# Gate taps of later blocks ahead of the gated products: a lead of up to six taps, three buffers for gated tiles, and one group's conv units a block earlier

## The chip, the cores and the metric

The kernel runs on one core of a Trainium2 chip. Its engines are called here by their full names and, in rows, by short ones: TensorE (PE, with PEld for the loading of weights), VectorE (DVE), ScalarE (ACT), GpSimd (POOL) and SyncE (SP), which issues most transfers. The metric is the device time of one execution in microseconds (us), as the median of several executions.

## The reference

For 8 sequences of 4224 positions and 192 channels in float32, the reference does two things one after the other.

```python
# 1: every head (24 channels) is averaged over 7 positions with its own softmax weights
out = np.einsum('hk,bskhg->bshg', softmax(weight), windows(x))
# 2: on that result, a causal filter of 5 taps per channel makes a gate
for k in range(5):
    gate_pre += conv_w[k] * xp[:, k:k + S, :]
gate = 1 / (1 + exp(-gate_pre))
val = x @ w_val                     # 192 x 192
return (gate * val) @ w_out         # 192 x 192
```

Every position thus needs the averaged x, four multiply-adds and one multiplication for the gate, a product with w_val, a multiplication by the gate, and a product with w_out.

## The kernel before

**Data.** The channels lie on the partitions, 128 of them in "main" tiles and the remaining 64 of two streams of sequences in a "third" tile, so that a block of 502 positions (a few have 448, 500, 304, 302 or 188) is one tile of 128 x 2 x 502 (x1, index 0 and 1) and one of 128 x 502 (x2, index 2). There are 36 blocks, n = 0 to 35. They come in 14 groups; groups 4 to 11 have three blocks each (blocks 8 to 31), group 12 is blocks 32 and 33, group 13 is blocks 34 and 35.

**Conv units.** The 7-position average of a group is made by TensorE as products with a band matrix (`conv_unit`, L312), four windows to a unit. ScalarE copies a unit's PSUM bank to SBUF (tile `e`, L321), and SyncE then scatters it into the group's x1 and x2 (L350). The list `todo` says how many units the loop does at the end of block n: 4, 3, 3 in the three blocks of a group (4 in blocks 8, 11, 14, 17, 20, 23), and 2 in each of blocks 26 to 31; none later. The last six units, those of group 13, stand in blocks 29 to 31.

**A block.** All engines follow the order in which the code is written. In block n:
- TensorE: `diagonal` (L447) starts v of the third tile and o of block n-1's third tile, `main` (L457) starts v of tiles 0 and 1, `columns` (L485) ends v and o of the third tile, `rows` (L470) ends v of tiles 0 and 1 and starts o of tiles 0 and 1 of block n-1, `main` ends those, and then the conv units follow. v is the product with w_val, o the product with w_out. All are computed from a high and a low part of each operand, except for `columns`.
- VectorE: four taps (L391) on the gate accumulator `pa` of block n+1 (128 x 1004), then the three gated products (L504: v times gate, third tile first, then tiles 0 and 1), then four taps on `pb` of block n+1 (128 x 502).
- ScalarE: it closes a gate accumulator (`gate_close`, sigmoid from PSUM to SBUF, L404) and opens the next one in the same bank (`gate_open`, first tap, L384); it casts x and the gated products to their high parts (L412, L420; GpSimd subtracts for the low parts, L413, L421); it copies o out (`project`, L520), and the conv units (L321).

**Buffers.** The accumulators `pa` and `pb` have one buffer each: taps of a gate can start only after ScalarE has closed the one before and opened it. The gated tiles have two buffers (`gp`). All other PSUM tiles share five banks (`ps`): in a block these are v of tile 2, o of tile 2, v of 0, v of 1, o of 0, o of 1 and one per conv unit, asked for in this order. A bank comes free when ScalarE has copied a unit or an o tile, or when VectorE has made the gated product from a v tile.

Of the kernel before, what the change touches and what calls it, by code (L numbers as in the profile page):

```python
# [17 lines left out]
NH, KW, HC, KG = 8, 7, 24, 5  # L18
# [42 lines left out]
NG = len(NJS)  # L61
# [13 lines left out]
N = len(STEPS)  # L75
# [19 lines left out]

HEAD = 4

SOON = {2: (0, 2), 3: (1, 3), 4: (3, 5), 5: (5, 8)}


@with_exitstack
def kernel(
# [12 lines left out]
    ep = ctx.enter_context(tc.tile_pool(name="ep", bufs=EBUFS))  # L115
    xp = ctx.enter_context(tc.tile_pool(name="xp", bufs=3))
    sp = ctx.enter_context(tc.tile_pool(name="sp", bufs=2))
    gp = ctx.enter_context(tc.tile_pool(name="gp", bufs=2))
    pp = ctx.enter_context(tc.tile_pool(name="pp", bufs=2))
    op = ctx.enter_context(tc.tile_pool(name="op", bufs=3))  # L120
    ps_g = ctx.enter_context(tc.tile_pool(name="ps_g", bufs=1, space=PSUM))
# [10 lines left out]
    for g, n in enumerate(NJS):  # L132
        k = PER_LOAD[n]
# [164 lines left out]
    def conv_unit(u):  # L298
        g, q, ws = units[u]
        n = NJS[g]  # L300
        if u == first_unit[g]:
            x1s[g] = xp.tile([128, 2 * XB], F32, tag="x1", name=f"x1_{g}")
            x2s[g] = xp.tile([128, XC], F32, tag="x2", name=f"x2_{g}")
        if ws[0] == (0, 0):
            es[g, q] = ep.tile([M, 4 * NMAX * WIN], F32, tag="e", name=f"e_{g}_{q}")
        e = es[g, q]
        pc = ps.tile([128, 512], F32, tag="p", name=f"pc_{u}")
        for k, (hi, j) in enumerate(ws):
            h = QUADS[q][hi]
            i, at = home[g, h]  # L310
            c = (at * n + j) * M
            nc.tensor.matmul(  # L312
                pc[:M, k * WIN : (k + 1) * WIN],
                lhsT=xtiles[i][:, c : c + M],
                rhs=band[:, 4 * q + hi, :],
                start=True,
                stop=True,
            )
        a = (ws[0][0] * n + ws[0][1]) * WIN
        w = len(ws) * WIN  # L320
        nc.scalar.copy(e[:, a : a + w], pc[:M, :w])  # L321
        done = [hi for hi, j in ws if j == n - 1]
        for hi in done:
            h = QUADS[q][hi]
            i, at = home[g, h]
            last = at == len(loads[i][1]) - 1
            if last and g >= BY_POOL:
                load_x(allowed(i))
            scatter(g, h, e[:, hi * n * WIN : (hi + 1) * n * WIN])
            if last and g < BY_POOL:  # L330
                load_x(allowed(i))
# [33 lines left out]
    def views(n, k=KG - 1):  # L365
        g, o, m = STEPS[n]
        b = second(NJS[g])
        x1v = x1s[g][:, : 2 * b].rearrange("p (a t) -> p a t", a=2)
        return x1v[:, :, o + k : o + k + m], x2s[g][:, o + k : o + k + m]
# [5 lines left out]
    def gate_open(n, i):  # L375
        if n >= N:
            return
        m = STEPS[n][2]
        if i == 0:
            acc = ps_g.tile([128, 2, 512], F32, tag="pa", name=f"pa_{n}")[:, :, :m]  # L380
        else:
            acc = ps_h.tile([128, 512], F32, tag="pb", name=f"pb_{n}")[:, :m]
        accs[n, i] = acc
        nc.scalar.mul(acc, views(n, 0)[i], cwt[:, i, 0:1])  # L384

    def gate_taps(n, i, k0=1, k1=KG):
        if n >= N:
            return
        acc = accs[n, i]
        for k in range(k0, k1):  # L390
            nc.vector.scalar_tensor_tensor(  # L391
                out=acc, in0=views(n, k)[i], scalar=cwt[:, i, k : k + 1],
                in1=acc, op0=ALU.mult, op1=ALU.add,
            )

    def gate_close(n, i):
        if n >= N:
            return
        m = STEPS[n][2]
        if i == 0:  # L400
            dst = g1s[n] = gp.tile([128, 2, MB], F32, tag="g1", name=f"g1_{n}")[:, :, :m]
        else:
            dst = g2s[n] = gp.tile([128, MB], F32, tag="g2", name=f"g2_{n}")[:, :m]
        nc.scalar.activation(dst, accs.pop((n, i)), AF.Sigmoid)  # L404
# [3 lines left out]
    def split1(pool, tag, n, x):  # L408
        m = STEPS[n][2]
        h = pool.tile([128, 2, MB], F32R, tag="h", name=f"{tag}h_{n}")[:, :, :m]  # L410
        l = pool.tile([128, 2, MB], F32R, tag="l", name=f"{tag}l_{n}")[:, :, :m]
        nc.scalar.copy(h, x)  # L412
        nc.gpsimd.tensor_tensor(out=l, in0=x, in1=h.bitcast(F32), op=ALU.subtract)  # L413
        return h, l
# [11 lines left out]
    def bank(what, n, q):  # L426
        t = ps.tile([128, 512], F32, tag="p", name=f"{what}_{n}_{q}")[:, : STEPS[n][2]]
        banks[what, n, q] = t
        return t

    def operands(what, n):
        return (w_val, *xs[n, 1], *xs[n, 2]) if what == "v" else (w_out, *pr[n, 1], *pr[n, 2])

    def parts(w, h, l):
        return (w.h, h), (w.l, h), (w.h, l)

    def ok(n):
        return 0 <= n < N

    def diagonal(what, n):  # L440
        if not ok(n):
            return
        acc = bank(what, n, 2)
        w, _, _, h2, l2 = operands(what, n)
        r = slice(W22, W22 + 128)
        for i, (a, b) in enumerate(parts(w, h2, l2)):
            nc.tensor.matmul(acc, lhsT=a[:, r], rhs=b, start=(i == 0), stop=False)  # L447

    def main(what, n, q):
        if not ok(n):  # L450
            return
        fresh = (what, n, q) not in banks
        acc = bank(what, n, q) if fresh else banks[what, n, q]
        w, h, l, _, _ = operands(what, n)
        r = slice(W11, W11 + 128)
        for i, (a, b) in enumerate(parts(w, h, l)):
            nc.tensor.matmul(  # L457
                acc, lhsT=a[:, r], rhs=b[:, q], start=(fresh and i == 0), stop=(not fresh and i == 2)
            )
# [14 lines left out]
    def columns(what, n):  # L474
        if not ok(n):
            return
        m = STEPS[n][2]
        acc = banks[what, n, 2]
        w = w_val if what == "v" else w_out
        x = views(n)[0] if what == "v" else g1s[n]  # L480
        cuts = [m * i // 4 for i in range(5)]
        for i in range(4):
            c = slice(cuts[i], cuts[i + 1])
            for q, p in enumerate(HALVES):
                nc.tensor.matmul(  # L485
                    acc[p, c], lhsT=w.f[:, W12 : W12 + 64], rhs=x[:, q, c],
                    start=False, stop=(i == 3),
                )

    def split(n):  # L490
        if n >= N:
            return
        x1, x2 = views(n)
        if n == 0:
            xs[n, 2] = split2(sp, "x", n, x2)
        xs[n, 1] = split1(sp, "x", n, x1)
        if n > 0:
            xs[n, 2] = split2(sp, "x", n, x2)

    def gated(n, q):  # L500
        if not ok(n):
            return
        v = g1s[n][:, q] if q < 2 else g2s[n]
        nc.vector.tensor_tensor(out=v, in0=banks.pop(("v", n, q)), in1=v, op=ALU.mult)  # L504

    def split_gated1(n):
        if ok(n):
            pr[n, 1] = split1(pp, "p", n, g1s[n])

    def split_gated2(n):  # L510
        if ok(n):
            pr[n, 2] = split2(pp, "p", n, g2s[n])
# [22 lines left out]
    def conv(k):  # L535
        for _ in range(k):
            if done[0] < len(units):
                conv_unit(done[0])
                done[0] += 1

    todo = [0] * (N + 1)
    for g in range(LAG, NG):
        a, b = SOON.get(g) or (first[g - LAG], first[g - 1])
        k = first_unit[g + 1] - first_unit[g]
        for i in range(k):
            todo[a + i * (b - a) // k] += 1
# [24 lines left out]
    for n in range(HEAD):  # L571
        k = 2 if n < 2 else 3
# [21 lines left out]
        now = todo[n] if n == 0 else todo[n] // 2  # L594
# [6 lines left out]
        gate_close(n + 1, 1)  # L601
        gate_open(n + 2, 1)

    for n in range(HEAD, N + 1):
        diagonal("v", n)
        gate_taps(n + 1, 0, 1, 3)
        split(n + 1)
        diagonal("o", n - 1)
        main("v", n, 0)
        main("v", n, 1)  # L610
        gate_taps(n + 1, 0, 3, KG)
        columns("v", n)
        gated(n, 2)
        gate_close(n + 1, 0)
        gate_open(n + 2, 0)
        columns("o", n - 1)
        split_gated2(n)
        project(n - 1, 2)
        rows("v", n)
        gated(n, 0)  # L620
        gated(n, 1)
        rows("o", n - 1)
        split_gated1(n)
        main("o", n - 1, 0)
        gate_taps(n + 1, 1)
        project(n - 1, 0)
        main("o", n - 1, 1)
        project(n - 1, 1)
        conv(todo[n])
        gate_close(n + 1, 1)  # L630
        gate_open(n + 2, 1)


# [89 lines left out]
```

## Time and profile before

| what | value |
|---|---|
| median of 3 runs | 390.54 us (390.15 to 391.44) |
| the profiled execution: its time, its span | 393.35 us, 391.6 us |
| TensorE clock granted, mean | 0.991 |
| busy: PE, PEld, DVE, ACT, POOL | 97%, 82%, 87%, 83%, 65% |
| chain that ended last: PE, DVE, DMA, ACT | 72%, 13%, 5%, 4% |
| HBM read and written | 29.34 MB, 26.00 MB |

The span runs from the first to the last instruction of the profiled execution; 1.75 us of its time lie outside the span. The ends of matmuls are modelled and a matmul that follows another closely overlaps it, so a busy TensorE is not a TensorE at its peak, and a wait of a few tenths shows as longer records rather than as a gap. In rows of the timeline the first number is the start, the second the time to the end of the last of the instructions merged, and the bracket tells how long the engine was idle before and what ended that.

### The profile page before, as it was taken

The page shows a single profiled execution, that of the slowest core. Times are in us where ns is not written, and L with a number is a line of the kernel's source. Part 1 is how long each engine was busy: PE and PEld are TensorE (multiplying, and loading weights), DVE is VectorE, ACT ScalarE, POOL GpSimd, SP SyncE. Part 2 cuts the span into 40 slices and gives each one's busy share as a digit, 9 for nine tenths or more (in the row PEclk, how much of TensorE's full clock was granted, in tenths as well). Part 3 has the DMA queues.
Part 4 walks back from the last instruction along what each step waited for, and adds up shares of the span by engine and source line. Part 5 has one row for each costly group of instructions (what it writes and reads, how often), then busy time and mean ns, then how long its engine had stood idle before and what let it go on. Part 6 is the DMA issues. An engine that isn't in the chain of part 4 may idle for free.

```text
span 391.6 us, 8620 instructions
## 1 busy us (share of the span) xinstructions
PE 378.0 (97%) x3204; PEld 321.6 (82%) x3204; DVE 342.3 (87%) x424; ACT 323.8 (83%) x525; POOL 254.8 (65%) x177
## 2 busy tenths in 40 slices
PE   8699999999999999999999999999999999999895
PEld 8687988898888888888888888888888787788684
DVE  4669899888998998998999899899899999999970
ACT  7458888988888888888889988888888888887863
POOL 1959765566667665666665666766566676776871
PEclk9969999999999999999999999999999999999999
DMA  8777869998687689778868868758987644333223
GB/s 293 210 195 223 253 214 290 258 239 272 210 251 216 180 260 256 210 217 253 224 194 256 219 185 261 218 178 253 257 226 227 211 160 146 114 135 133 80 106 144
DMA packets 38209, 82.49 MB, mean 211 GB/s; under 512 B 4856, under 2 KB 17528, under 8 KB 38168
## 3 DMA queue, kind: packets, MB, share of 16 engines
q1 hardware_dynamic: 36720, 79.90, 67.6%
q0 software_dynamic: 896, 1.31, 1.4%
q10 hardware_dynamic: 552, 0.73, 0.6%
q8 instruction: 25, 0.41, 0.5%
q14 instruction: 16, 0.13, 0.1%
HBM read 29.34 MB, written 26.00 MB: 141 GB/s over the span
## 4 chain that ended last, share of the span: by engine, by line
PE 72%; DVE 13%; DMA 5%; ACT 4%; issue 3%; SPq 2%; POOL 0%; DVEq 0%; ACTq 0%
PE pc L312 20%; PE o L457 10%; PE v L457 9%; PE v L485 7%; PE v L470 6%; PE o L485 6%; DVE pa L391 6%; PE o L470 5%; PE o L447 5%; PE v L447 4%; DVE pb L391 4%; DVE g L504 3%; DMA x<-e 2%; DMA x<-xw 2%; DMA scr<-wv 1%
## 5 line engine op out<-in xcount | busy, mean ns | idle before, releaser
L391 DVE SCALAR_TENSOR_TENSOR pa<-x,cwt,pa 128x1004 f32<-128x1004 f32 (+5 forms) x144 | 172.9, 1201 | 10.7 <-ACT pa L384 6.8
L413 POOL TENSOR_TENSOR xl<-x,xh 128x1004 fp32r<-128x1004 f32 (+5 forms) x36 | 74.8, 2077 | 73.1 <-ACT xh L412 58.9
L312 PEld LDWEIGHTS pc<-band,x 128*120 128x120 f32 x912 | 103.1, 187 | 7.1 <-issue 3.9
L312 PE MATMUL pc<-band,x 128*120 128x122 f32 x912 | 104.2, 272 | 4.3 <-DMA x<-xw 3.8
L391 DVE SCALAR_TENSOR_TENSOR pb<-x,cwt,pb 128x502 f32<-128x502 f32 (+5 forms) x144 | 102.2, 710 | 3.8
L413 POOL TENSOR_TENSOR pl<-g,ph 128x1004 fp32r<-128x1004 f32 (+5 forms) x36 | 79.4, 2204 | 10.3 <-ACT ph L412 7.7
L504 DVE TENSOR_TENSOR g<-v,g 128x502 f32<-128x502 f32 (+5 forms) x108 | 65.8, 642 | 21.1 <-PE v L470 16.1
L404 ACT ACTIVATE g<-pa 128x1004 f32<-128x1004 f32 (+5 forms) x36 | 34.5, 959 | 38.8 <-DVE pa L391 21.1
L321 ACT COPY e<-pc 120x488 f32<-120x488 f32 x114 | 59.1, 586 | 6.4 <-PE pc L312 6.3
L421 POOL TENSOR_TENSOR pl<-g,ph 128x502 fp32r<-128x502 f32 (+5 forms) x36 | 43.0, 1194 | 32.8 <-ACT ph L420 32.7
L520 ACT COPY ot<-o 128x502 f32<-128x502 f32 (+5 forms) x108 | 56.2, 551 | 3.3 <-PE o L457 2.6
L421 POOL TENSOR_TENSOR xl<-x,xh 128x502 fp32r<-128x502 f32 (+5 forms) x36 | 41.8, 1162 | 0.0
L384 ACT ACTIVATE pa<-x,cwt 128x1004 f32<-128x1004 f32 (+5 forms) x36 | 37.8, 1051 | 4.8 <-DMA x<-e 3.7
L485 PEld LDWEIGHTS v<-x,wvf 128*64 128x64 f32 x576 | 29.1, 136 | 11.8 <-issue 11.4
L485 PE MATMUL v<-x,wvf 128*64 128x125 f32 (+4 forms) x576 | 37.2, 270 | 0.0
L412 ACT CAST ph<-g 128x1004 fp32r<-128x1004 f32 (+5 forms) x36 | 35.1, 976 | 1.5 <-DVE g L504 1.5
L485 PE MATMUL o<-g,wof 128*64 128x125 f32 (+4 forms) x576 | 35.6, 264 | 0.0
L412 ACT CAST xh<-x 128x1004 fp32r<-128x1004 f32 (+5 forms) x36 | 34.6, 961 | 0.0
L485 PEld LDWEIGHTS o<-g,wof 128*64 128x64 f32 x576 | 30.9, 136 | 0.1
L457 PE MATMUL o<-ph,woh 128*128 128x502 f32 (+5 forms) x72 | 30.9, 429 | 0.0
L457 PE MATMUL v<-xh,wvh 128*128 128x502 f32 (+5 forms) x72 | 27.2, 377 | 0.3 <-ACT e L321 0.3
L457 PE MATMUL v<-xh,wvl 128*128 128x502 f32 (+5 forms) x72 | 27.1, 377 | 0.0
(75 smaller groups left out, 573.1 us busy)
## 6 DMA issues: line engine op xcount, KB each, us to landing
x<-xw SPq DMA_DIRECT2D x64, 300.0 KB
out<-ot SPq DMA_DIRECT2D x24, 753.0 KB
x<-e SPq DMA_DIRECT2D x40, 285.9 KB
x<-xw SPq DMA_DIRECT2D x20, 360.0 KB
out<-ot SPq DMA_DIRECT2D x8, 672.0 KB
x<-e SPq DMA_DIRECT2D x32, 141.6 KB
x<-e SPq DMA_DIRECT2D x25, 171.6 KB
x<-e SPq DMA_DIRECT2D x16, 94.4 KB
```

Source lines behind the costliest of these rows:

```text
L312: nc.tensor.matmul(pc[:M, k * WIN : (k + 1) * WIN], lhsT=xtiles[i][:, c : c + M], rhs=band[:, 4 * q + hi, :], start=True, stop=True,)
L321: nc.scalar.copy(e[:, a : a + w], pc[:M, :w])
L384: nc.scalar.mul(acc, views(n, 0)[i], cwt[:, i, 0:1])
L391: nc.vector.scalar_tensor_tensor(out=acc, in0=views(n, k)[i], scalar=cwt[:, i, k : k + 1], in1=acc, op0=ALU.mult, op1=ALU.add,)
L412: nc.scalar.copy(h, x)
L413: nc.gpsimd.tensor_tensor(out=l, in0=x, in1=h.bitcast(F32), op=ALU.subtract)
L421: nc.gpsimd.tensor_tensor(out=l, in0=x, in1=h.bitcast(F32), op=ALU.subtract)
L457: nc.tensor.matmul(acc, lhsT=a[:, r], rhs=b[:, q], start=(fresh and i == 0), stop=(not fresh and i == 2))
L470: nc.tensor.matmul(acc, lhsT=a[p, r], rhs=b[p], start=(fresh and i == 0), stop=(not fresh and i == 2))
L485: nc.tensor.matmul(acc[p, c], lhsT=w.f[:, W12 : W12 + 64], rhs=x[:, q, c], start=False, stop=(i == 3),)
L504: nc.vector.tensor_tensor(out=v, in0=banks.pop(("v", n, q)), in1=v, op=ALU.mult)
L520: nc.scalar.copy(ots[n][:, q * m : (q + 1) * m], banks.pop(("o", n, q)))
```

## The change

VectorE's order from block 5 on is now a list of taps that runs through all later gates (third tile's taps behind main tiles' taps), and a table LEAD says how many taps beyond `pa` of block n+1 are done before the gated products of block n: none up to block 8, 1 from block 9, 2 from 11, 3 from 12, 4 from 14, 5 from 17, 6 from 21, then 5, 6, 5 in blocks 28, 29 and 30, 3 from 32, 1 in 33, 0 from 34. The products so move behind up to four taps of `pb` of block n+1 and two of `pa` of block n+2.

A gate whose four taps are written is pending, and `flush` closes it and opens the next one. ScalarE's order thus changes too: `flush` stands behind the third product, behind the casts of the products, and, for `pa`, between the first or second conv unit and the rest. The rule on COST and FITS only decides which taps are written in the block's lower half, and with them where the pending gate is flushed. Gated tiles have three buffers in place of two. The six conv units of the last group stand a block earlier, so block 28 has 4 units, 29 and 30 have 2 and 31 has none.

```diff
+LEAD = {0: 0, 9: 1, 11: 2, 12: 3, 14: 4, 17: 5, 21: 6, 28: 5, 29: 6, 30: 5, 32: 3, 33: 1, 34: 0}
+COST, FITS = (1.3, 0.78), 4.6
...
-    gp = ctx.enter_context(tc.tile_pool(name="gp", bufs=2))
+    gp = ctx.enter_context(tc.tile_pool(name="gp", bufs=3))
...
         a, b = SOON.get(g) or (first[g - LAG], first[g - 1])
+        if g == NG - 1:
+            a, b = a - 1, b - 1
...
+    T = KG - 1
+    taps = [(n, i, k) for n in range(HEAD + 1, N) for i in range(2) for k in range(1, KG)]
+    at_tap = [0]
+    pending = []
+
+    def flush(*which):
+        for n, i in [p for p in pending if p[1] in which]:
+            gate_close(n, i)
+            gate_open(n + 1, i)
+            pending.remove((n, i))
+
+    def tap():
+        n, i, k = taps[at_tap[0]]
+        at_tap[0] += 1
+        flush(*(j for m, j in pending if m < n and j == i))
+        gate_taps(n, i, k, k + 1)
+        if k == T:
+            pending.append((n, i))
+
+    def ahead(n):
+        lead = LEAD[max(k for k in LEAD if k <= n)]
+        return min(2 * T * (n - HEAD) + T + lead, len(taps))
+
     for n in range(HEAD, N + 1):
         diagonal("v", n)
-        gate_taps(n + 1, 0, 1, 3)
         split(n + 1)
         diagonal("o", n - 1)
         main("v", n, 0)
         main("v", n, 1)
-        gate_taps(n + 1, 0, 3, KG)
+        while at_tap[0] < ahead(n):
+            tap()
         columns("v", n)
         gated(n, 2)
-        gate_close(n + 1, 0)
-        gate_open(n + 2, 0)
+        flush(0)
         columns("o", n - 1)
...
         split_gated1(n)
+        flush(1)
         main("o", n - 1, 0)
-        gate_taps(n + 1, 1)
+        used = first_used = 0
+        while at_tap[0] < ahead(n + 1):
+            _, i, k = taps[at_tap[0]]
+            if used + COST[i] > FITS:
+                break
+            used += COST[i]
+            tap()
+            if (i, k) == (0, T):
+                first_used = used
         project(n - 1, 0)
         main("o", n - 1, 1)
         project(n - 1, 1)
-        conv(todo[n])
-        gate_close(n + 1, 1)
-        gate_open(n + 2, 1)
+        now = min(todo[n], 2 if first_used > 3.5 else 1 if first_used else 0)
+        conv(now)
+        flush(0)
+        conv(todo[n] - now)
+        flush(1)
```

**ScalarE in block 22**, where the lead is six. In these rows ph2_22 and ph_22 are the casts of block 22's gated products, ot_21 the copies of o, e the copies of conv units 89, 90 and 91, g2_23 and g1_24 the closing of gates, pb_24 and pa_25 the opening of the next. Before, the main gate is turned over ahead of the casts and the third tile's gate behind all conv copies:

```order
L404 ACTIVATE g1_23_3125<-pa_23_3010 128x1004
L384 ACTIVATE pa_24_3127<-x1_9_2557,cwt_155 128x2x502
L420 CAST ph2_22_3137<-g2_22_3084 128x502
L520 COPY ot_21_3141<-o_21_2_3102 128x502
L412 CAST ph_22_3159<-g1_22_3008 128x1004
L520 COPY ot_21_3141<-o_21_0_3151 128x502
L520 COPY ot_21_3141<-o_21_1_3152 128x502
L321 COPY e_10_1_3068<-pc_89_3176 120x488
L321 COPY e_10_1_3068<-pc_90_3185 120x488
L321 COPY e_10_1_3068<-pc_91_3194 120x488
L404 ACTIVATE g2_23_3203<-pb_23_3086 128x502
L384 ACTIVATE pb_24_3205<-x2_9_2558,cwt_155 128x502
```

The same stretch of ScalarE in the changed program:

```order
L424 CAST ph2_22_3143<-g2_22_3052 128x502
L524 COPY ot_21_3147<-o_21_2_3110 128x502
L416 CAST ph_22_3165<-g1_22_2953 128x1004
L408 ACTIVATE g2_23_3169<-pb_23_3054 128x502
L388 ACTIVATE pb_24_3171<-x2_9_2566,cwt_155 128x502
L524 COPY ot_21_3147<-o_21_0_3157 128x502
L524 COPY ot_21_3147<-o_21_1_3158 128x502
L325 COPY e_10_1_3082<-pc_89_3186 120x488
L408 ACTIVATE g1_24_3195<-pa_24_3080 128x1004
L388 ACTIVATE pa_25_3197<-x1_9_2565,cwt_155 128x2x502
L325 COPY e_10_1_3082<-pc_90_3199 120x488
L325 COPY e_10_1_3082<-pc_91_3208 120x488
```

Both turnovers now stand between the cast of the main product and the copy of the second unit: that of `pb` ahead of the o copies, that of `pa` behind the first unit. So it is in blocks 21 to 27 and 29; in blocks 17 to 20, 28 and 30 the turnover of `pa` stands behind the second unit, and in blocks up to 13 both are where they were.

**VectorE from block 16 to block 17**, where the lead goes from four to five. Before, the products of a block follow the four taps on `pa` of the next:

```order
L504 TENSOR_TENSOR g2_16_2346<-v_16_2_2350,g2_16_2346 128x502
L504 TENSOR_TENSOR g1_16_2270<-v_16_0_2368,g1_16_2270 128x502
L504 TENSOR_TENSOR g1_16_2270<-v_16_1_2372,g1_16_2270 128x502
L391 SCALAR_TENSOR_TENSOR pb_17_2348<-x2_7_1820,cwt_155,pb_17_2348 128x502 x4
L391 SCALAR_TENSOR_TENSOR pa_18_2389<-x1_7_1819,cwt_155,pa_18_2389 128x2x502 x4
L504 TENSOR_TENSOR g2_17_2465<-v_17_2_2469,g2_17_2465 128x502
```

In the changed program nine taps lie between them in place of eight, and they belong to later gates:

```order
L508 TENSOR_TENSOR g2_16_2312<-v_16_2_2353,g2_16_2312 128x502
L508 TENSOR_TENSOR g1_16_2274<-v_16_0_2369,g1_16_2274 128x502
L508 TENSOR_TENSOR g1_16_2274<-v_16_1_2373,g1_16_2274 128x502
L395 SCALAR_TENSOR_TENSOR pa_18_2393<-x1_7_1821,cwt_155,pa_18_2393 128x2x502 x4
L395 SCALAR_TENSOR_TENSOR pb_18_2431<-x2_7_1822,cwt_155,pb_18_2431 128x502 x4
L395 SCALAR_TENSOR_TENSOR pa_19_2503<-x1_7_1821,cwt_155,pa_19_2503 128x2x502
L508 TENSOR_TENSOR g2_17_2429<-v_17_2_2472,g2_17_2429 128x502
```

The products of block 17 moved behind `pb_18` and the first tap of `pa_19`; that tap needs ScalarE to have closed `pa_18` and opened `pa_19`, which stand behind block 16's conv copies and the casts of x of block 18.

**TensorE from the end of block 22** keeps its order. Its waits are shown in brackets:

```order
L316 MATMUL pc_90_3199<-band_91,x_70_2949 120x122 [waits DVE_49]
L316 MATMUL pc_91_3208<-band_91,x_71_2963 120x122 [waits DVE_49]
L451 MATMUL v_23_2_3217<-xh2_23_3106,wvh_157 128x502 [waits Activation_49]
L451 MATMUL o_22_2_3229<-ph2_22_3143,woh_161 128x502 [waits Activation_49]
L461 MATMUL v_23_0_3233<-xh_23_3102,wvh_157 128x502 [waits Activation_49]
L461 MATMUL v_23_1_3237<-xh_23_3102,wvh_157 128x502 [waits Activation_49]
```

The last two rows read the same xh_23 and each waits for ScalarE anew, so the second wait is for a bank. At v_23_1 the five tiles asked for last are pc_90, pc_91, v_23_2, o_22_2 and v_23_0; the last three are still being written, and pc_91 is copied behind pc_90: v_23_1 takes the bank of pc_90, when ScalarE has copied that unit.

## The prediction

> **What bounds the kernel now.** I read the page first (busy shares), then the windows, to see whether one engine is the bound all the way, then the waits of TensorE and VectorE, and last the timelines of one block. The windows are block 9 to block 26, block 26 to block 34, and the rest; columns are start and end, length, then busy time of PE, PEld, DVE, ACT and POOL.
>
> ```profile
> 121.65:301.12 179.47, 179.47 (x1506) 151.66 (x1504) 165.67 (x188) 156.63 (x244) 117.42 (x69) 1.00 0.77 224
> 301.12:376.97 75.85, 74.03 (x596) 58.97 (x594) 73.05 (x89) 64.07 (x103) 53.88 (x33) 1.00 0.42 143
> ```
>
> Up to block 26 TensorE has no gap at all: 179.47 of 179.47 us, while VectorE rests 13.8 us and ScalarE 22.8. From block 26 on VectorE is nearly as full as TensorE (73.05 and 74.03 of 75.85). So there are two stretches: one in which VectorE has a little to spare, and a tail in which it is late. The waits say who is late. The first row is VectorE's over the whole span, the next three are those of TensorE's weight loads from 301 to 371 us.
>
> ```profile
> DVE g L504 <- PE v L470: 16.1, 26, 1.1
> ...
> PEld o L470 <- DVE g L504: 3.6, 6, 1.1
> ...
> PEld o L447 <- POOL pl L421: 0.9, 1, 0.9
> PEld o L447 <- ACT ph L420: 0.3, 1, 0.3
> ```
>
> VectorE waits for v, 26 times, before the products of tiles 0 and 1. TensorE waits in the tail: 3.6 + 0.9 + 0.3 = 4.8 us, which is most of what this change can win there. In VectorE's timeline, the bracket is the wait for v at the head of blocks 9, 10, 11, 12, 14, 17, 21 and 23:
>
> ```profile
> 121.65 1.27 DVE L504 TENSOR_TENSOR g<-v,g 128x502 f32<-128x502 f32 x2 [0.98 <-PE v L470]
> 122.83 3.08 DVE L391 SCALAR_TENSOR_TENSOR pb<-x,cwt,pb 128x502 f32<-128x502 f32 x4
> 125.82 5.17 DVE L391 SCALAR_TENSOR_TENSOR pa<-x,cwt,pa 128x1004 f32<-128x1004 f32 x4
> 130.90 0.67 DVE L504 TENSOR_TENSOR g<-v,g 128x502 f32<-128x502 f32 x1
> 131.94 1.27 DVE L504 TENSOR_TENSOR g<-v,g 128x502 f32<-128x502 f32 x2 [0.36 <-PE v L470]
> 142.32 1.27 DVE L504 TENSOR_TENSOR g<-v,g 128x502 f32<-128x502 f32 x2 [0.46 <-PE v L470]
> 153.42 0.68 DVE L504 TENSOR_TENSOR g<-v,g 128x502 f32<-128x502 f32 x1 [1.02 <-PE v L470]
> 174.03 0.68 DVE L504 TENSOR_TENSOR g<-v,g 128x502 f32<-128x502 f32 x1 [0.40 <-PE v L470]
> 205.79 1.27 DVE L504 TENSOR_TENSOR g<-v,g 128x502 f32<-128x502 f32 x2 [0.42 <-PE v L470]
> 248.70 1.27 DVE L504 TENSOR_TENSOR g<-v,g 128x502 f32<-128x502 f32 x2 [1.06 <-PE v L470]
> 269.34 1.27 DVE L504 TENSOR_TENSOR g<-v,g 128x502 f32<-128x502 f32 x2 [0.47 <-PE v L470]
> ```
>
> I call the start of such a row T0 of its block. VectorE's own round, from T0 to the end of the next third-tile product, is 130.90 + 0.67 - 121.65 = 9.92 us; a pb tap takes 0.75 us (2.99 / 4), a pa tap 1.27 to 1.29. The wait is about 1.0 us behind a block with four conv units and about 0.4 behind one with three. I take 0.42 of it as the floor, since it hardly falls below that, and so the spare time as the wait less 0.42: about 0.6 in a round behind four units, nothing in the others.
>
> **The change part by part.** It removes and adds no work: the same taps, products, copies and matmuls run. Three things move: ScalarE's turnovers, VectorE's products, and the six units of the last group.
>
> *First, ScalarE's turnovers (TensorE's banks).* Before, in block 24 (T0 = 280.48 us), ScalarE did this, then TensorE's conv units and the main v of blocks 25 and 24:
>
> ```profile
> 279.57 1.01 ACT L404 ACTIVATE g<-pa 128x1004 f32<-128x1004 f32 x1 [1.44 <-PE o L485]
> 280.62 1.10 ACT L384 ACTIVATE pa<-x,cwt 128x1004 f32<-128x1004 f32 x1
> 281.66 0.59 ACT L420 CAST ph<-g 128x502 fp32r<-128x502 f32 x1
> 282.16 0.57 ACT L520 COPY ot<-o 128x502 f32<-128x502 f32 x1
> 282.63 1.03 ACT L412 CAST ph<-g 128x1004 fp32r<-128x1004 f32 x1
> 283.56 1.05 ACT L520 COPY ot<-o 128x502 f32<-128x502 f32 x2
> 284.50 1.52 ACT L321 COPY e<-pc 120x488 f32<-120x488 f32 x3
> 285.87 0.64 ACT L404 ACTIVATE g<-pb 128x502 f32<-128x502 f32 x1
> 286.54 0.68 ACT L384 ACTIVATE pb<-x,cwt 128x502 f32<-128x502 f32 x1
> 287.16 1.01 ACT L412 CAST xh<-x 128x1004 fp32r<-128x1004 f32 x1
> ...
> 282.44 2.68 PE L312 MATMUL pc<-band,x 128*120 128x122 f32 x24
> ...
> 287.01 0.39 PE L457 MATMUL v<-xh,wvh 128*128 128x502 f32 x1
> ...
> 276.08 0.39 PE L457 MATMUL v<-xh,wvh 128*128 128x502 f32 x1
> ...
> 276.75 0.39 PE L457 MATMUL v<-xh,wvh 128*128 128x502 f32 x1
> ```
>
> The copies end at 286.02, and v of tile 1, which takes the second unit's bank, starts at 287.01 (T0 + 6.53): 0.99 us of slack. Now, where the lead is six, both turnovers stand behind the cast of the main product and ahead of the second copy. The cast can start when the products are made, T0 + 1.27. From there, start to start: cast 0.93 (282.63 to 283.56), close pb 0.67, open pb 0.62, two o copies 0.94, first unit 0.46 (a third of 284.50 to 285.87), close pa 1.05, open pa 1.04, and the second copy with its whole duration:
>
> ```profile
> L321 ACT COPY e<-pc 120x488 f32<-120x488 f32 x114 | 59.1, 586 | 6.4 <-PE pc L312 6.3
> ```
>
> 0.93 + 0.67 + 0.62 + 0.94 + 0.46 + 1.05 + 1.04 + 0.59 = 6.30, so the bank is free at T0 + 7.57 and TensorE wants it at T0 + 6.53. That is a wait of 1.04 us which nothing takes back, as TensorE has no gap. Blocks 21, 22, 24 and 25 pay it: 4.16. Block 23 has four units; its banks move on by one, and v of tile 0 takes the second unit's at 276.08 (T0 = 269.34, so T0 + 6.74): 0.83. In blocks 20 and 28 the turnover of pa stands behind the second of four units, so v of tile 1 (T0 + 7.41, from 276.75) waits for the third copy at 7.57 + 0.46 = 8.03: 0.62 each. Together 4.16 + 0.83 + 1.24 = **6.2 us**. If each release takes 0.1 us more than the rows show, it is 7; if the slack seen before holds (some other order of arrival), it is 0.
>
> The Trainium skill (Perfetto Trace Analysis, Matmuls) says that independent matmul groups should rotate through PSUM banks so that the emptying of one overlaps the next group's matmuls. The trace of before agrees (286.02 against 287.01), and this change works against the rule; by it alone this term would stand as worked out above.
>
> *Second, the ramp.* Whenever the lead grows by a tap, one round of VectorE has nine taps and the products are late by what the spare time doesn't hold. TensorE feels it: the third-tile product frees the bank for o of tile 1, and the o rows wait. These rows show the delay in block 27, where VectorE's round of 9.92 met a TensorE round of 9.40 (300.85 to 310.25):
>
> ```profile
> 300.85 0.39 PE L470 MATMUL o<-ph,woh 64*128 64x502 f32 x2
> ...
> 310.25 0.39 PE L470 MATMUL o<-ph,woh 64*128 64x502 f32 x1
> 311.11 0.49 PE L470 MATMUL o<-ph,woh 64*128 64x502 f32 x1 [0.47 <-DVE g L504]
> ...
> 311.99 0.50 PE L457 MATMUL o<-ph,woh 128*128 128x502 f32 x1
> ...
> 280.19 0.40 PE L470 MATMUL o<-ph,woh 64*128 64x502 f32 x2
> ...
> 280.98 0.49 PE L457 MATMUL o<-ph,woh 128*128 128x502 f32 x1
> ```
>
> From the first o row to the next line took 1.74 us there and 0.79 in block 24, so being late costs TensorE directly. A pb tap more in block 9 costs 0.75 - (0.98 - 0.42) = 0.19, in block 11 0.75 - 0.04 = 0.71, in block 12 0.75 - 0.60 = 0.15, in block 14 0.75. In block 17 it is a pa tap, 1.29 without spare time. That tap needs ScalarE to have opened pa_19: from T0 of block 16, VectorE's four pa and four pb taps end at 1.27 + 5.17 + 2.99 = 9.4; ScalarE, on its chain above with three copies and without the turnover of pa, is through at 1.27 + 0.93 + 0.67 + 0.62 + 0.94 + 1.37 = 5.8, casts the next x (some 0.9 and 0.5, as it does the products) and turns pa over in 2.09, to 9.3. The two meet, and I add nothing: 1.29. In block 21 the pa tap is held by 0.64 of spare time and by the 0.62 that TensorE lost in block 20. Sum: 0.19 + 0.71 + 0.15 + 0.75 + 1.29 = **3.1 us**; at least 0, if other slack takes it, at most 4.4 (with the 1.29 of block 21).
>
> *Third, the tail.* Block 27 stands behind two units as before, at the same lead, so it stays 0.95 late, and the opening of pa adds about 0.35: 1.3. In block 28 one tap less and four units free it, 29 and 30 come out even. Block 31 is 9.92 - 9.40 = 0.5 late. Blocks 32 and 33 stand behind blocks without units: TensorE's round there is 9.40 less two units,
>
> ```profile
> 303.09 1.84 PE L312 MATMUL pc<-band,x 128*120 128x122 f32 x16
> 304.69 0.47 PE L447 MATMUL v<-xh,wvh 128*128 128x502 f32 x1
> ```
>
> 1.60, so 7.8, and VectorE's 9.92 less two pb taps, 8.4: 0.6 late, and once more nearly the same, at 448 columns, in block 33: 1.2. What stays is 1.3 + 0.5 + 1.2 = 3.0 of the 4.8: a gain of **1.8 us**, with bounds 0 and 4.8. The third buffer of the gated tiles costs nothing, as no wait for one shows in any of the views above, and the earlier units of the last group only bring their copies forward.
>
> The sum is 6.2 + 3.1 - 1.8 = +7.5 us. The profiled execution took 393.35 us (its span of 391.6 and 1.75 around it) and would take 400.9; it lies 2.8 us above the median of the three runs, 390.54. I put the same 7.5 on the median: 398.0.
>
> **The rivals.** *Running ahead pays (faster).* TensorE's waits of the tail go, and the turnovers find room: if the copy's real release is 1.0 us earlier than my chain, the first term is nothing (that is the point from which it decides), the ramp hides in waits, and up to 4.8 us is won: 385.7 to 389. For it speaks that VectorE rests 13.8 us before block 26 and is short in the tail; against it, that no rest of it is longer than 1.06 us at a time and that my chain adds durations that stand in the trace. The Trainium skill (Perfetto Trace Analysis, Optimization Strategy) says that a kernel with several regimes may gain by interleaving them. The trace shows two such regimes, and by that rule the time would be about 385.7; whether it pays no run shows yet.
>
> *Only one of the two losses is real.* Either ScalarE's chain holds and the ramp is covered, 6.2 - 1.8 = +4.4, or the ramp costs and the banks do not, 3.1 - 1.8 = +1.3. Times 391.8 to 394.9. For it speaks that a wait of TensorE in one place lends VectorE spare time in the next.
>
> *Nothing moves in sum.* Gain and loss are equal to within 1.2 us, and the time is about 390.5. That needs a tail gain near its upper bound against one small loss.
>
> **How the numbers follow.** All three terms as worked out: 0.58, time 398.0, its own range 395 to 402. Only one loss: 0.18. Within 0.3% of before (1.2 us either way, about what a measurement of this kernel can tell from no change): 0.08. Faster: 0.16. The range leaves out the faster case and little above: 389.5 to 402. Faster 0.16, within 0.3% 0.08, slower 0.76.
>
> **What would show it.** Right, if TensorE shows new waits for ScalarE's copies (line of `e`) at the main v after blocks 20 to 25, about 1 us each, so that the stretch from block 20 to 26 grows by some 6 us; if the o rows of blocks 11, 14 and 17 wait for the gated products; and if the tail's waits for the products shrink only by half. In ScalarE's rows the second copy should end about 7.6 us behind T0. Wrong, if the copies end by T0 + 6.5 or TensorE's stretch from block 9 to 26 keeps its 179.5 us: then the first two terms fall. Wrong in the other way, if VectorE waits for the opening of pa by more than 0.3 us a block: then the rounds of VectorE set the time, and it goes above 402.

## The result and the profile after

| | before | changed |
|---|---|---|
| median | 390.54 us (389.77 to 391.44, 5 runs) | 400.70 us (399.48 to 401.13, 5 runs) |
| ratio, 95% interval | | 1.0248 (1.0224 to 1.0273) |
| profiled execution: time, span | 393.35 us, 391.6 us | 401.13 us, 399.0 us |

The change costs 10.2 us by the medians, and 8.7 to 10.7 by the interval of the ratio. The two profiled spans differ by 7.4 us only, because their starts differ: before, TensorE waited 3.8 us for its first x in the profiled execution, and 2.2 us after, and an early stretch at a granted clock of 0.50 lasted 6.83 us before (from 19.36) and 3.41 after (from 18.35). So the two traces are compared from block 8 on. The marks are the T0 of blocks 8, 20, 26 and 34, the start of the products of tiles 0 and 1 (where a row of the timeline holds all three products, T0 lies 1.27 us, the length of these two, ahead of its end). The profiled execution of one kernel further down, the one with its fourth tap in block 21, ran at a granted clock of 0.66 throughout (520.95 us) and is left out: that kernel's stages come from one more execution of 389.58 us, and its median of 389.02 would be 388.96 without the slow one. First the windows of before from block 8 to 20 and 20 to 26 (the third, 75.85 us, stands in the prediction), with the columns as there:

```profile
110.74:237.53 126.79, 126.79 (x1067) 107.37 (x1065) 116.89 (x133) 110.58 (x173) 83.14 (x49) 1.00 0.78 225
237.53:301.12 63.59, 63.59 (x536) 53.71 (x534) 58.49 (x67) 55.45 (x87) 41.50 (x25) 1.00 0.78 228
```

The same three stretches of the changed kernel:

```profile
107.83:237.55 129.72, 128.46 (x1068) 107.27 (x1066) 119.99 (x137) 113.74 (x175) 81.69 (x48) 1.00 0.75 219
237.55:307.11 69.56, 64.95 (x536) 52.88 (x534) 59.97 (x67) 56.41 (x88) 42.33 (x26) 1.00 0.75 212
307.11:384.45 77.34, 74.03 (x596) 59.38 (x594) 67.61 (x82) 63.27 (x100) 53.52 (x34) 0.98 0.40 139
```

The ramp lost 2.93 us, the six rounds at full lead 5.97, the tail 1.49: 10.39 in all, close to the 10.2 of the medians. TensorE had no gap up to block 26 before; now it rests 1.26 and 4.61 us in the first two stretches, and VectorE has more done in the second, not less. Who it waits for, by the weight loads, in the ramp, at full lead and in the tail (three answers of the view of waits):

```profile
PEld o L474 <- DVE g L508: 2.5, 3, 1.3
...
PEld v L461 <- ACT e L325: 7.1, 6, 1.3
...
PEld o L474 <- DVE g L508: 2.2, 1, 2.2
...
PEld v L451 <- POOL xl L425: 1.2, 1, 1.2
PEld o L451 <- POOL pl L425: 1.1, 2, 0.6
PEld v L461 <- ACT e L325: 0.9, 1, 0.9
```

In the ramp it is the gated products, at full lead ScalarE's copies of conv units, once a round in six rounds. Block 24, shown in the prediction as it was, now reads like this on ScalarE, from T0 = 284.34, and below it TensorE's main v of tiles 0 and 1:

```profile
285.64 1.03 ACT L416 CAST ph<-g 128x1004 fp32r<-128x1004 f32 x1 [1.24 <-DVE g L508]
286.58 0.58 ACT L408 ACTIVATE g<-pb 128x502 f32<-128x502 f32 x1
287.19 0.68 ACT L388 ACTIVATE pb<-x,cwt 128x502 f32<-128x502 f32 x1
287.82 1.04 ACT L524 COPY ot<-o 128x502 f32<-128x502 f32 x2
288.75 0.58 ACT L325 COPY e<-pc 120x488 f32<-120x488 f32 x1
289.21 1.03 ACT L408 ACTIVATE g<-pa 128x1004 f32<-128x1004 f32 x1
290.27 1.10 ACT L388 ACTIVATE pa<-x,cwt 128x1004 f32<-128x1004 f32 x1
291.31 1.02 ACT L325 COPY e<-pc 120x488 f32<-120x488 f32 x2
```

```profile
290.65 0.38 PE L461 MATMUL v<-xl,wvh 128*128 128x502 f32 x1
291.92 0.49 PE L461 MATMUL v<-xh,wvh 128*128 128x502 f32 x1 [0.88 <-ACT e L325]
```

The second copy starts at 291.31 and, with 0.56 us for one, ends at T0 + 7.5; v of tile 1 starts 0.05 us behind that, at T0 + 7.58 in place of T0 + 6.53. The bracket shows 0.88 us of the 1.05, as the matmul ahead of it covers the rest.

In the tail the new loss sits in two rounds, behind blocks 26 and 27. In block 26 VectorE waits for x, and TensorE then for the product. ScalarE's opening of pa ahead of that tap, which reads the same x, also comes after 1.08 us of idle time, for which the profile names no cause. The first row is VectorE's, the second ScalarE's, the others TensorE's:

```profile
315.23 1.27 DVE L395 SCALAR_TENSOR_TENSOR pa<-x,cwt,pa 128x1004 f32<-128x1004 f32 x1 [1.37 <-DMA x<-e]
...
314.09 1.10 ACT L388 ACTIVATE pa<-x,cwt 128x1004 f32<-128x1004 f32 x1 [1.08 <-issue]
...
318.43 0.56 PE L474 MATMUL o<-ph,woh 64*128 64x502 f32 x1 [1.76 <-DVE g L508]
318.44 0.97 PE L474 MATMUL o<-ph,wol 64*128 64x502 f32 x2
```

The windows behind that wait show what followed. The granted clock, third from the end, is 0.56 in the mean from 318.43 to 322.31, and it is 0.50 in the 3.41 us from 318.72 to 322.13:

```profile
318.43:322.31 3.88, 3.88 (x12) 2.69 (x13) 3.84 (x5) 3.76 (x6) 3.88 (x4) 0.56 0.01 4
318.72:322.13 3.41, 3.41 (x11) 2.27 (x10) 3.37 (x5) 3.29 (x6) 3.41 (x4) 0.50 0.00 0
```

### The profile page after: what moved, and what is told of

Read it like the earlier page. It is cut to its first block, busy times and chain, and to the rows that moved or that the text cites. A ratio compares the mean times of both kernels' runs of the same rounds, so it can differ in the third digit from the quotient of the medians.

```text
span 399.0 us, 8634 instructions
## 1 busy us (share of the span) xinstructions
PE 379.5 (95%) x3204; PEld 319.6 (80%) x3204; DVE 341.3 (86%) x424; ACT 327.2 (82%) x525; POOL 253.9 (64%) x177
## 4 chain that ended last, share of the span: by engine, by line
PE 61%; ACT 15%; DVE 10%; DMA 8%; issue 3%; SPq 1%; POOL 0%; DVEq 0%; POOLq 0%; ACTq 0%
PE pc L316 15%; PE o L461 8%; PE v L461 8%; PE v L489 7%; PE v L474 6%; DMA x<-e 6%; PE o L489 6%; DVE pa L395 4%; PE o L474 4%; DVE g L508 4%; PE o L451 3%; ACT g L408 3%; PE v L451 3%; ACT pa L388 3%; ACT e L325 3%
## 5 line engine op out<-in xcount | busy, mean ns | idle before, releaser
L325 ACT COPY e<-pc 120x488 f32<-120x488 f32 x114 | 61.0, 572 | 7.7 <-PE pc L316 7.2
L424 ACT CAST ph<-g 128x502 fp32r<-128x502 f32 (+5 forms) x36 | 20.9, 581 | 17.1 <-DVE g L508 15.6
L461 PE MATMUL v<-xh,wvh 128*128 128x502 f32 (+5 forms) x72 | 28.0, 389 | 5.4 <-ACT e L325 5.4
```

What stands on the lines that cost most here:

```text
L461: nc.tensor.matmul(acc, lhsT=a[:, r], rhs=b[:, q], start=(fresh and i == 0), stop=(not fresh and i == 2))
```

## The experiments

Each kernel is the changed one with the edit shown; "before" ran beside it on the same chip. "Stages" is what the three stretches (block 8 to 20, 20 to 26, 26 to 34) took over those of before, worked out as above from the T0 of one profiled execution of each kernel. What a single round lost, as told below, is the same difference between the T0 of two blocks that follow each other; the rounds that an edit leaves alone mostly agree to a few hundredths of a us.

| kernel | median, us | before, us | ratio (95%) | stages, us |
|---|---|---|---|---|
| the change | 400.70 | 390.54 | 1.0248 (1.0224 to 1.0273) | +2.93, +5.97, +1.49 |
| two copies first | 397.74 | 390.82 | 1.0175 (1.0136 to 1.0213) | +2.94, +3.63, -0.14 |
| lead four | 391.66 | 390.82 | 1.0023 (0.9999 to 1.0047) | +1.42, -0.04, -0.56 |
| no lead | 393.77 | 390.82 | 1.0075 (1.0049 to 1.0102) | +0.47, -0.04, +1.66 |
| lead four, ramp behind four units | 391.01 | 390.82 | 1.0005 (0.9984 to 1.0026) | +0.34, +0.01, -0.54 |
| ... and own tail | 389.92 | 390.93 | 0.9972 (0.9947 to 0.9998) | +0.24, +0.03, -1.42 |
| ramp behind four, units back | 391.18 | 390.93 | 1.0013 (0.9994 to 1.0032) | +0.24, +0.06, -0.27 |
| no lead, units back | 392.11 | 390.93 | 1.0037 (1.0010 to 1.0064) | +0.44, -0.02, +0.03 |
| five in blocks 26 and 27 | 398.70 | 390.93 | 1.0207 (1.0169 to 1.0244) | +2.89, +6.18, -1.50 |
| back each round | 389.51 | 391.03 | 0.9965 (0.9944 to 0.9987) | +0.24, +0.01, -2.02 |
| ... and fourth tap in block 21 | 389.02 | 391.03 | 0.9949 (0.9926 to 0.9972) | -0.09, +0.22, -2.03 |

**Is it the bank?** One number moves pa's turnover behind the second unit's copy.

```diff
-        now = min(todo[n], 2 if first_used > 3.5 else 1 if first_used else 0)
+        now = min(todo[n], 2 if first_used else 0)
```

> One number changes: where the lead is six, the turnover of pa stands behind the second unit's copy instead of the first. Theory (v of tile 1 waits for the bank of the second unit): that bank is free 2.09 us earlier, so TensorE's weight loads wait for ScalarE's copies under 2 us in all, after 9.1 with the change; VectorE waits some 0.46 us longer for the opening of pa in each such round, which takes back about 0.4 in rounds with three units. Net about 2 to 3 us off: 398 to 399. Rival (the late products or the opening of pa set the time, and the wait for the bank only lies on top): no gain, 400.5 to 402.

Measured 397.74. At full lead (block 20 to 26) TensorE's waits for the copies fall from 7.1 to 2.1 us and VectorE's for the opening of pa rise; the first row is TensorE's weight loads, the second VectorE, which stood at 1.6 us with the change:

```profile
PEld v L461 <- ACT e L325: 2.1, 2, 1.5
...
DVE pa L395 <- ACT pa L388: 4.0, 5, 0.8
```

That is the trade the theory named: that stage costs 3.63 in place of 5.97. So the bank is what TensorE waited for, and at lead six neither of the two places tried is free: ahead of the copy TensorE waits, behind it VectorE does. The gain of 3.0 us by the medians is at the upper edge of the 2 to 3 expected. The waits over the whole span, expected under 2 us, stay at 4.1: 2.1 in blocks 20 and 23 and 0.9 behind block 28, all three with four units, and the rest ahead of block 20.

**Is it the sixth and fifth tap?** The lead stops at four, so pa is turned over behind all copies.

```diff
-LEAD = {0: 0, 9: 1, 11: 2, 12: 3, 14: 4, 17: 5, 21: 6, 28: 5, 29: 6, 30: 5, 32: 3, 33: 1, 34: 0}
+LEAD = {0: 0, 9: 1, 11: 2, 12: 3, 14: 4, 32: 3, 33: 1, 34: 0}
```

> The lead stops at four, so no tap of pa of block n+2 stands ahead of the products and pa is turned over behind all copies. Theory: the bank waits of blocks 20 to 27 (6.0 us and more) and the pa tap of block 17 (1.3) go, the ramp of four pb taps (about 1.9) stays, the tail gives back 1 to 2 us: 390 to 392.5. Rival (running ahead costs in itself, through late products in every round): 396 or more.

Measured 391.66, and TensorE has no gap in the second stretch again:

```profile
107.25:235.46 128.21, 127.79 (x1068) 107.39 (x1066) 119.12 (x137) 113.64 (x175) 83.79 (x49) 1.00 0.76 222
235.46:299.01 63.55, 63.55 (x536) 53.66 (x534) 58.51 (x66) 55.70 (x87) 41.50 (x24) 1.00 0.82 228
```

The four taps that lie in pb cost 1.42 us to build and nothing to hold. The two in pa cost the other 1.5 us of the ramp and the whole 6 us behind it. Of these two the fifth, too, was held at no cost: in the changed kernel the rounds behind blocks 18 and 19, at lead five with the turnover of pa behind the second copy, took 0.01 us less each than before. So the cost behind the ramp came with the sixth.

**Is the ramp the taps?** The lead of four grows only behind blocks with four units.

```diff
+LEAD = {0: 0, 9: 1, 12: 2, 15: 3, 18: 4, 32: 3, 33: 1, 34: 0}
```

> The lead stops at four and grows only in blocks 9, 12, 15 and 18, each behind a block with four conv units, where VectorE waited about 1.0 us. Theory (a tap costs what the spare time doesn't hold): 0.15 to 0.2 us a tap, some 0.7 in place of 1.9, so 1 to 1.5 us under the kernel with lead four: 388.5 to 391. Rival (the ramp's 2.9 us come from ScalarE's changed order, not from the taps): the same as with lead four, within 0.4 us.

Measured 391.01, just above the range, and 0.65 us under the kernel with lead four by the medians, where 1 to 1.5 were expected; the intervals overlap. The stage shows the difference more clearly, 0.34 in place of 1.42 us in one trace of each. Up to block 17 it lies within 0.1 us of before, and the 0.3 us come at block 19. The rival falls: ScalarE runs the same orders in both kernels and keeps the last one from there on, only the block in which a tap is taken up differs.

**What is left without a lead?**

```diff
+LEAD = {0: 0}
```

> LEAD is zero throughout; what stays of the change is the third buffer of gated tiles, the new place of the flushes, and the last group's units a block earlier. Theory: as before within 0.3%, 389.5 to 391.5. Rival (the earlier units of the last group cost the 1 to 2 us that the tail lost): 392 or more.

This missed, and the rival was right: 393.77, 1.0075 of before. The stage table puts 1.66 of it in the tail, and the round behind block 28, where two more units stand, lost 1.70. TensorE's row behind block 31, which has no units now:

```profile
360.11 0.60 PE L474 MATMUL o<-ph,woh 64*128 64x502 f32 x1 [1.71 <-DVE g L508]
```

And the window that follows, with the mean granted clock third from the end:

```profile
360.11:362.00 1.89, 1.89 (x6) 1.14 (x7) 1.85 (x4) 1.86 (x3) 0.17 (x1) 0.56 0.00 0
```

The work moved away from there is not won back: TensorE waits 1.71 us for VectorE instead. With the units back where they were:

```diff
-        if g == NG - 1:
-            a, b = a - 1, b - 1
```

> No lead, and the last group's units back: of the change only the third buffer and the place of the flushes stay. Theory: the 1.6 us that the stage table of the kernel without lead shows at block 29 go, and the time is within 0.4 us of 1 to 1.5 us under that kernel, 391 to 392.4. Rival (the third buffer or the flushes cost it): 393.5 or more.

Measured 392.11, tail +0.03: the 1.6 us were the units. In the ramp 0.36 us are lost behind block 8, won back behind block 9 and lost again behind block 10, from ScalarE's order or the buffers; which of them was not tried, and the rest of the 1.2 us by the medians lies outside the stages or inside the interval (0.4 to 2.5 us).

**Are the units' places worth 1.6 us at a lead of four too?** Two edits together, the lead grown behind four units and the units back:

> As the kernel whose lead of four grows behind four units (391.0), but with the last group's units back in blocks 29 to 31. Theory (the two units moved into block 28 lengthen a round of TensorE by 1.6 us while VectorE idles, and the shorter round after block 31 gives nothing back since VectorE sets that one): 1.6 us less, 389.4, 388.6 to 390. Rival (the place of the units does not matter): 391 again.

Measured 391.18, against 391.01 with the units moved. This missed: here their place does not matter in sum. The moved units cost 1.7 us behind block 28 here too, but now taps given back in blocks 32 and 33 shorten VectorE's rounds where TensorE's are short as well, and 0.74 and 1.54 us come back. With the units back the same taps meet TensorE's longer rounds and win 0.3 us. So what a moved unit costs seems to depend on whether VectorE has taps to give back in the round that the unit leaves.

**The two rounds behind blocks 26 and 27.**

```diff
+LEAD = {0: 0, 9: 1, 11: 2, 12: 3, 14: 4, 17: 5, 21: 6, 26: 5, 29: 6, 30: 5, 32: 3, 33: 1, 34: 0}
```

> The changed kernel with one number changed: lead five in place of six in blocks 26 and 27. Theory (in block 26 the sixth tap needs group 11's x a block early; VectorE waits 1.4 us for the scatter, TensorE then 1.8 us, and its clock falls to 0.56 for the next 3.9 us): the wait for the transfer and the low clock go, the rounds after blocks 26 and 27 lose less by 2 to 3 us in all, 397.5 to 399. Rival (those rounds lose their time to the bank waits, which stay): 400 or more.

Measured 398.70. VectorE's first tap on the x of group 11 still stands in block 26, but it has no wait ahead of it:

```profile
314.45 1.26 DVE L395 SCALAR_TENSOR_TENSOR pa<-x,cwt,pa 128x1004 f32<-128x1004 f32 x1
```

And the tail, in the window from block 26 to 34, has its clock back:

```profile
306.50:380.85 74.35, 72.81 (x596) 58.48 (x594) 68.58 (x84) 63.05 (x100) 53.56 (x34) 1.00 0.42 144
```

77.34 became 74.35, and the rounds behind blocks 26 and 27 lose nothing (-0.14 and 0.00) where the change lost 1.33 and 1.50. With six taps ahead VectorE reached that tap at T0 + 6.75 and waited for its x until T0 + 8.12; with five one tap more of pa stands ahead of it, it comes at T0 + 7.95, and its x is there. The bank waits are not the cause, as TensorE's one wait for a unit's copy in this stretch (0.9 us) stands behind block 28. The trace of the kernel with two copies first shows the first loss without the second: there a wait for the opening of pa still cost the round behind block 26 1.08 us, but the clock stayed at 1.00, and the round behind block 27 lost nothing.

**Giving the lead back.** First one tap each in blocks 27, 29, 31 and 33 with the units back, then three in blocks 27, 28 and 29, then the fourth tap taken up later:

```diff
+LEAD = {0: 0, 9: 1, 12: 2, 15: 3, 18: 4, 27: 3, 29: 2, 31: 1, 33: 0}
...
+LEAD = {0: 0, 9: 1, 12: 2, 15: 3, 18: 4, 27: 3, 28: 2, 29: 1, 33: 0}
...
+LEAD = {0: 0, 9: 1, 12: 2, 15: 3, 21: 4, 27: 3, 28: 2, 29: 1, 33: 0}
```

> Lead of four pb taps grown behind blocks with four units (9, 12, 15, 18), the last group's units back where they were before the change, and the lead given back a tap at a time in blocks 27, 29, 31 and 33. Theory (from block 26 on VectorE's rounds of about 9.9 us set the pace against TensorE's 9.4, so each pb tap given back is worth up to 0.75 us, and the ramp costs 0.4): 390.8 + 0.4 - 3.0 = 388.2, 387.5 to 389. Rival (the tail is held by something else, ScalarE's casts or GpSimd's low parts): 390 to 391.5.

> As the kernel with its own tail (389.9), but three taps are given back in blocks 27, 28 and 29, one a round, and the last in block 33. Theory (each round from block 26 on has VectorE some 0.5 us over TensorE; a tap given back every round takes that away each time, while one given back every other round is used up only in part): the loop gains 3 x 0.5 + 0.7 less 0.3 for the ramp, 1.9 us, against 1.2: 389.0 to 389.6. Rival (any order of giving back is worth the same): 389.9 again.

> As the kernel that gives a tap back every round, but the fourth tap of lead is taken up in block 21, where VectorE waited 1.06 us for v, and not in block 18. Theory: the 0.28 us that the loop lost at block 19 go, 388.7 to 389.4. Rival (the loss at block 19 is that of ScalarE's new place for the turnover of pa and comes with the fourth tap wherever it stands): as with block 18, within 0.1 us in the stage table.

> The kernel that takes up its fourth tap in block 21 once more, for its profile, since the one before shows TensorE at a clock of 0.66 from end to end. Theory: from block 8 to block 26 its stage table stays within 0.1 us of before, and at the end of the loop it lies 2.0 us under it. Rival: 0.3 us are lost again, at block 22.

Measured 389.92, 389.51 and 389.02. The first won less than half of what was expected (1.0 of 2.6 us by the medians), and VectorE's rows of block 29 show why:

```profile
327.38 0.67 DVE L508 TENSOR_TENSOR g<-v,g 128x502 f32<-128x502 f32 x1
329.00 1.27 DVE L508 TENSOR_TENSOR g<-v,g 128x502 f32<-128x502 f32 x2 [0.95 <-PE v L474]
```

With a tap given back the products are early and wait 0.95 us for TensorE, most likely because TensorE had been held up in the round without one. Given back in three rounds running, each is worth 0.37 to 0.41 us (rounds behind blocks 26 to 28), and the one in block 33 0.73. The step from the first to the second is inside the intervals of the medians; the stages show it, -1.42 against -2.02. The last kernel has the lowest median, 0.9949 (0.9926 to 0.9972) of before, though its interval overlaps that of the one ahead of it. In its trace the loss at block 19 is gone and 0.3 us appear at block 22, of which 0.1 come back in the next round: from block 8 to 26 it lies 0.14 us over before, against 0.25, so its rival, which had the loss return, is right for the larger part.

## Why the prediction was right, and where a term was off

The forecast was 398.0 (389.5 to 402.0) and slower by 7.5 us; it is 400.7, slower by 10.2.

*First term, 6.2 us: right, block by block.* The chain of 6.30 us behind the main product was worked out from before, and it ended at T0 + 7.57 there and T0 + 7.5 in the trace. The rounds behind blocks 20 to 25 lost 0.73, 1.13, 1.03, 0.95, 1.14 and 0.99 us, forecast 0.62, 1.04, 1.04, 0.83, 1.04 and 1.04. TensorE's waits stand where the prediction put them: in block 20 at T0 + 8.05 (forecast 8.03), in block 23 at T0 + 7.58 (forecast 7.57). The round behind block 28 lost 2.07; the two moved units cost 1.70 there in the kernel without a lead, and 0.37 remain for the forecast 0.62.

*Second term, 3.1 us: right in sum, 2.93.* By blocks 9, 11, 12, 14 and 17: 0.05, 0.64, 0, 0.69 and 1.58, forecast 0.19, 0.71, 0.15, 0.75 and 1.29. The pa tap of block 17 cost 0.3 more than its own duration. The meeting of VectorE and ScalarE there was even, as forecast: ScalarE's opening ended at 203.29 and the tap started at 203.32, 0.09 behind the tap before it. Where the 0.3 come from stays open.

*Third term, a gain of 1.8 us: it came out as a loss of 1.5.* The step that failed is "Block 27 stands behind two units as before, at the same lead, so it stays 0.95 late, and the opening of pa adds about 0.35". That 0.35, for which the prediction shows no row, was mis-sized: the rounds behind blocks 26 and 27 lost 1.33 + 1.50 = 2.83 us more than before. With six taps ahead VectorE reaches the x of group 11 in block 26, a block earlier than in the order of before and 1.37 us before it has landed, and I followed which engine a moved step passes but not when its data land. The low clock behind that wait was in no term. The 2.5 us between 2.83 and 0.35 are nearly the whole distance to the measured time (2.7). Without these 2.83, and without the 0.37 that belong to the first term, the tail gave 2.83 + 0.37 - 1.49 = 1.71 us, where the forecast without its 0.35 was 2.15. That they are so near is partly luck: the 1.71 already hold the 1.70 that the moved units cost behind block 28, which the prediction put at nothing, so the other rounds of the tail gave 3.4.

*"The earlier units of the last group only bring their copies forward"* was wrong: without a lead they cost 1.6 us. At a lead of four it did not show in the sum, since the taps given back in the tail paid for it; at the leads of the changed kernel the units were not tried in their old place.

*The rivals.* Both losses were real (2.93 and 5.97 us), so the rival of only one falls, and the interval shuts out the one that nothing moves. Running ahead pays, but only a smaller change of the same kind shows it: up to four taps, which need no second turnover of pa ahead of the copies, won 2.0 us by the medians. The Trainium skill's rule on regimes (Perfetto Trace Analysis, Optimization Strategy) agrees with that kernel, though its 2.0 us are less than half of the 4.8 which I gave for it. The Trainium skill's rule on rotating banks (Perfetto Trace Analysis, Matmuls) agrees with the stretch at full lead: there the emptying of a bank came too late for the next matmuls, at 7.1 us of waits.

## What to carry to other kernels

When an engine is made to run ahead, look at what its earlier steps ask of the others: here each tap of the third tile was free to hold, and so was the first one of pa, but the sixth tap moved 2.1 us of ScalarE's work ahead of a copy that had been ready only 1 us before TensorE wanted its bank. Take up lead only in rounds where the engine waits (0.34 us for four taps against 1.42), and give it back in every round in which it is late, not in every other one. Check for each moved step not only which engine it passes but when the data that it reads have landed.

## What the runs showed of the hardware

Twice a wait of TensorE was followed by a low clock: 0.3 and 0.2 us behind the end of gaps of 1.76 us (the change, 318.43) and 1.71 us (no lead, 360.11) the granted clock fell to 0.50 for 3.41 us, and matmuls that follow each other at 0.23 us took 0.42. The round behind block 27 of the change lost 1.50 us with it. The round behind block 32 of the kernel without a lead lost none, as VectorE, which shows no wait from 351 to 376, set its length. Behind a gap of 1.22 us (two copies first, 317.40) the clock stayed at 1.00:

```profile
317.40 0.49 PE L474 MATMUL o<-ph,woh 64*128 64x502 f32 x1 [1.22 <-DVE g L508]
```

The Trainium skill (TensorE: Matmul & The Clock Gate, Part 1: The HAM clock gate) says that the clock is halved after at least one idle window of about 3.4 us and released after about as long a busy one. The release agrees (3.41 us in both traces); the idle time does not, as gaps of half that length came ahead of the fall here. Whether the windows' position or the lighter load before the gap decided it, no run shows.
